# Linear attention with ReGLU on one core: direct values for three tile pairs, Strassen for all keys, values one pair ahead of the keys

## The chip, the cores and the metric

The kernel runs on one core of one Trainium2 chip. The metric is the device time of one execution in microseconds, the smaller the better. PE is the matmul engine, DVE, ACT and POOL are the vector, scalar and general engines, SP issues most transfers. "Product" below means one of the seven products of a Strassen group.

## The reference

The input is 2048 tokens of 1024 features, in bf16. Cut to what matters:

```python
phi = lambda t: jnp.where(t > 0, t + 1, jnp.exp(t)) + 1e-6
qkv = layernorm(x) @ wqkv                       # 1024 -> 3 * 1024
pq, pk = phi(q), phi(k)                          # 32 heads of 32
kv = jnp.einsum("bhsd,bhse->bhde", pk, v)        # sums over all tokens
z = jnp.einsum("bhsd->bhd", pk)
o = num / den                                    # pq @ kv over pq @ z
h = x + o @ wo
# ... second layer norm, gate * relu, up, down: the later 84% of the span, untouched here
```

The change touches only the stage that makes keys and values of all tokens and accumulates `kv`. Queries cannot start before it ends.

## The kernel before

Tokens are taken in 16 tiles of 128, two tiles a pair, eight pairs. A projection of one pair to keys (or to values) is done in one of two ways. The direct way is 32 matmuls of 128x512. The other is one Strassen group: seven products of four matmuls each, 28 in all, bought with sums: four sums of the transposed input per pair on DVE (`x_sums`), and four sums of the weights, made once, on DVE for keys (`TWk`) and on POOL for values (`TWv`, 32 pieces that are put into POOL's queue a few at a time by `pool_piece`).

The group, cut to its order. `SX(i)` is an input sum, `TW(i)` a weight sum, and `hook(i)` a place where other work is issued:

```python
def sgroup(...):
    prod(a, X(0, 0), W(0, 0), True, "P1")
    ident_act(bank(b), bank(a), ...)             # ACT copies PSUM to PSUM
    hook(1)
    prod(f, SX(2), TW(2), True, "P7")            # second product: the first input sum
    ident_act(s7, bank(f), ...)
    hook(2)
    prod(b, SX(1), TW(1), False, "P6")           # third: the third input sum
    ident_act(bank(c), bank(b), ...)             # the fifth product waits for this copy
    hook(3)
    prod(a, X(1, 0), W(1, 0), False, "P2")
    hook(4)
    prod(c, SX(0), TW(0), False, "P5")
    hook(5)
    prod(b, X(1, 1), TW(3), False, "P4")         # sixth: the last weight sum
    hook(6)
    prod(c, SX(3), W(1, 1), False, "P3")
```

The input sums of a pair, four DVE operations with two inputs in SBUF each:

```python
def x_sums(p):
    ...
    add(2, xb(0, 0), xb(0, 1), ALU.subtract, ...)
    add(0, xb(0, 1), xb(1, 1), ALU.add, ...)
    add(1, s(0), xb(0, 0), ALU.subtract, ...)
    add(3, xb(1, 0), s(1), ALU.subtract, ...)
```

The order of the stage, cut. Tiles 0 to 3 get keys and values directly while their inputs and the weights arrive; then each pair gets its keys and at once its values, and the input sums of pair p+1 are made at the end of key group p:

```python
for p in range(WB // 2, NP_):                    # pairs 2 to 7
    def h_k3(p=p): ...  kvacc(st)                # accumulation of the pair before, behind the third product
    def h_k6(p=p, sq=sq):
        ...
        if p + 1 < NP_:
            x_sums(p + 1)                        # used by key group p + 1: a value group lies between
    k_group(p, {1: h_k1, 3: h_k3, 5: h_k5, 6: h_k6})
    if p == WB // 2:
        ...                                      # values of pair 2 directly
        continue
    v_group(p, {3: h_v3, 5: h_v5, 6: h_v6})      # h_v6: normalise two later tiles, transpose them by DMA
```

`kvacc` is the accumulation, 16 matmuls of 128x129 per pair. `W` and `TW` of keys and values live in the tiles that the profile calls `RAB`, `RC` (`TWk`) and `RW` (`TWv`); the transposed input is in `RAB`, the input sums in `RWG` and `RH`, copies in `RX` and `RXH`, keys, values and the input tiles in `RE`.

## Time and profile before

| | before |
|---|---|
| time, median of four runs (range) | 749.56 us (748.96 to 749.98) |
| span of the profiled run | 747.4 us |
| PE busy | 99% |
| first projection matmul | 8.30 us |
| first query group | 120.67 us |
| waits of PE over 0.3 us between these | one, 0.7 us |

These are the span, the engines' busy time, the clock that PE was granted (in tenths, per slice of the span) and the shares of the chain that ended last, from the page of the kernel before:

```profile
span 747.4 us, 10100 instructions
...
PE 737.0 (99%) x3547; PEld 337.8 (45%) x3603; DVE 537.3 (72%) x1067; ACT 299.9 (40%) x516; POOL 87.5 (12%) x148
...
PEclk9999999999999999999999999999999999999999
...
PE 89%; DVE 4%; ACT 3%; issue 2%; SPq 0%; DMA 0%; DVEq 0%; POOL 0%; ACTq 0%; POOLq 0%
```

PE sets the time: it is always busy, at the full clock, and 89% of the chain. So each matmul less is worth its spacing. What that is, a row of the timeline shows. These are PE's rows of one steady key group and the start of its value group, before the change (start, time, what; four matmuls make one product):

```profile
86.37 1.04 PE L604 MATMUL ps<-RAB,RH 128*128 128x512 bf16 x4
87.24 1.03 PE L604 MATMUL ps<-RAB 128*128 128x512 bf16 x4
88.11 2.00 PE L604 MATMUL ps<-RW,RWG 128*128 128x512 f16 x8
89.94 1.03 PE L604 MATMUL ps<-RAB 128*128 128x512 bf16 x4
```

From 86.37 to 87.24 there are four matmuls in 0.87 us. A single one is listed with 379 ns. The Trainium skill ("TensorE: Matmul & The Clock Gate", Back-to-back issue gap) gives, by its formula, about 216 ns from one 512-column matmul to the next at the full clock, and the trace agrees (the 131 ns that the section gives for a sustained stream do not appear here): the 379 ns is a latency that the next one overlaps.

The waits of PE in the stage, in us in total, number, and the longest:

```profile
PE ps L604 <- ACT RAB L731: 0.7, 1, 0.7
```

This is DVE at the same time as the PE rows above, the input sums (L806):

```profile
87.56 0.93 DVE L806 TENSOR_TENSOR RWG<-RAB 128x512 f16<-128x512 bf16 x2
88.52 0.43 DVE L806 TENSOR_TENSOR RWG<-RWG,RAB 128x512 f16<-128x512 f16 x1
88.98 0.42 DVE L806 TENSOR_TENSOR RH<-RAB,RWG 128x512 f16<-128x512 bf16 x1
```

They start 0.32 us after the value group's first product at 87.24, take about 0.45 us each, and are not wanted before the next key group near 94 us. These rows give least, median and greatest duration in ns of the input sums that started between 33 and 51 us, before:

```profile
L806 DVE TENSOR_TENSOR RWG<-RAB x4: 534/884/887, 33.9 to 47.4; 128x512 f16<-128x512 bf16 x4
L806 DVE TENSOR_TENSOR RWG<-RWG,RAB x2: 774/776/778, 35.6 to 48.4; 128x512 f16<-128x512 f16 x2
```

Here POOL adds weights almost without a pause, and one sum takes up to 0.89 us. A whole value projection lies between these sums and their use.

### The profile page before, as it was taken

How to read it: one execution, taken by the hardware profiler on the slowest of the kernel's cores; microseconds unless marked ns; L12 is line 12 of the kernel's file. 1: busy time of each engine (PE TensorE's matmuls, PEld its weight loads, DVE VectorE, ACT ScalarE, POOL GpSimd, SP SyncE). 2: the span in 40 equal slices, each digit the busy share in tenths (PEclk: the TensorE clock that was granted, in tenths of full speed). 3: DMA queues.
4: the chain of work that ended last, by engine and by line, in shares of the span. 5: the costliest groups of instructions: out<-in, count | busy, mean ns of one | idle time of the engine just before them, and what ended most of it. 6: DMA issues, size and time to landing. Idle time of an engine off the chain costs nothing.

```text
span 747.4 us, 10100 instructions
## 1 busy us (share of the span) xinstructions
PE 737.0 (99%) x3547; PEld 337.8 (45%) x3603; DVE 537.3 (72%) x1067; ACT 299.9 (40%) x516; POOL 87.5 (12%) x148
## 2 busy tenths in 40 slices
PE   8999999999999999999999999999999999999998
PEld 4444444344554444444444444444444444444443
DVE  7987875898776899887877485766867677563343
ACT  4367755665832354545443100035454454520000
POOL 2695440000350000000000010000000000000000
PEclk9999999999999999999999999999999999999999
DMA  9734115223898696565428799732323131036663
GB/s 306 200 74 97 29 29 184 84 29 82 219 224 243 222 290 198 172 187 175 143 85 251 224 266 301 234 120 84 105 65 112 58 114 56 1 87 182 211 192 132
DMA packets 160225, 113.38 MB, mean 152 GB/s; under 512 B 51504, under 2 KB 141360, under 8 KB 160176
## 3 DMA queue, kind: packets, MB, share of 16 engines
q1 hardware_dynamic: 160176, 112.75, 52.6%
q8 instruction: 28, 0.46, 0.3%
q14 instruction: 21, 0.17, 0.1%
HBM read 85.46 MB, written 15.73 MB: 135 GB/s over the span
## 4 chain that ended last, share of the span: by engine, by line
PE 89%; DVE 4%; ACT 3%; issue 2%; SPq 0%; DMA 0%; DVEq 0%; POOL 0%; ACTq 0%; POOLq 0%
PE ps L604 89%; DVE RAB L670 1%; ACT ps L609 1%; ACT RX L663 1%; ACT RX L609 1%; DVE RX L667 1%; DVE RE L1038 1%; ACT RXH L633 0%; ACT RXH L638 0%; DVE RX L884 0%; SPq L510 0%; DVE RXH L1062 0%; DMA RW<-in_B_W_down_dram 0%; DVE rden L1036 0%; PE ps L728 0%
## 5 line engine op out<-in xcount | busy, mean ns | idle before, releaser
L609 ACT ACTIVATE ps<-ps 128x512 f32<-128x512 f32 x150 | 87.4, 584 | 172.3 <-PE ps L604 155.6
L604 PE MATMUL ps<-RC,RO 128*128 128x512 f16 x672 | 154.4, 379 | 0.7 <-DVE RE L1219 0.6
L604 PE MATMUL ps<-RW,RAB 128*128 128x512 f16 (+1 forms) x681 | 150.1, 379 | 0.6
L604 PEld LDWEIGHTS ps<-RW,RAB 128*128 128x128 bf16 (+1 forms) x692 | 67.7, 98 | 81.6
L604 PE MATMUL ps<-RH,RWG 128*128 128x512 bf16 x435 | 103.0, 379 | 0.7
L604 PEld LDWEIGHTS ps<-RC,RO 128*128 128x128 f16 x672 | 65.5, 98 | 80.7 <-ACT ps L609 1.1
L609 ACT ACTIVATE RE<-ps 128x512 f32<-128x512 f32 x120 | 70.7, 597 | 75.0 <-PE ps L604 52.8
L604 PE MATMUL ps<-RC,RWG 128*128 128x512 f16 x296 | 70.7, 379 | 0.0
L604 PEld LDWEIGHTS ps<-RH,RWG 128*128 128x128 bf16 x448 | 43.8, 98 | 52.9 <-DVE RAB L1212 0.3
L1212 DVE TENSOR_TENSOR RAB<-ps,RAB 128x512 bf16<-128x512 f32 x28 | 19.3, 690 | 63.3 <-PE ps L604 63.3
L604 PE MATMUL ps<-RH,RO 128*128 128x512 bf16 (+1 forms) x242 | 58.3, 379 | 0.7
L609 ACT ACTIVATE RAB<-ps 128x512 bf16<-128x512 f32 x56 | 33.4, 597 | 61.9 <-PE ps L604 61.8
L604 PE MATMUL ps<-RAB 128*128 128x512 bf16 x239 | 56.6, 379 | 1.3 <-ACT RAB L731 0.7
L604 PE MATMUL ps<-RW,RE 128*128 128x512 bf16 x248 | 56.8, 379 | 0.8 <-DVE RXH L1062 0.4
L1143 DVE TENSOR_TENSOR RO<-RWG,RO 128x512 f16<-128x512 bf16 x108 | 45.5, 421 | 1.8
L604 PEld LDWEIGHTS ps<-RC,RWG 128*128 128x128 bf16 (+1 forms) x296 | 28.5, 98 | 35.7 <-ACT ps L609 2.2
L1143 DVE TENSOR_TENSOR RO<-RWG 128x512 f16<-128x512 bf16 x108 | 40.7, 418 | 2.8 <-DMA RWG<-in_B_W_up_dram 2.1
L625 POOL TENSOR_TENSOR rstd<-rstd,neghalf 128x1 f32<-128x1 f32 x20 | 12.6, 632 | 251.5 <-DVE rstd L622 251.5
L1219 DVE TENSOR_TENSOR RE<-ps,RE 128x512 f32<-128x512 f32 x56 | 38.3, 691 | 5.0 <-ACT RE L609 4.8
L1224 DVE TENSOR_TENSOR RE<-ps,RE 128x512 f32<-128x512 f32 x56 | 38.2, 683 | 0.0
L604 PEld LDWEIGHTS ps<-RH,RO 128*128 128x128 f16 (+1 forms) x256 | 24.6, 98 | 29.8 <-ACT RX L609 1.5
L667 DVE TENSOR_SCALAR RX<-RX 128x512 bf16<-128x512 bf16 x64 | 19.9, 311 | 24.0 <-ACT RX L663 23.9
(118 smaller groups left out, 809.9 us busy)
## 6 DMA issues: line engine op xcount, KB each, us to landing
RWG<-in_B_W_gate_dram SPq DMA_DIRECT2D x28, 512.0 KB, 3.7
RWG<-in_B_W_up_dram SPq DMA_DIRECT2D x28, 512.0 KB, 4.9
RW<-t_scr SPq DMA_DIRECT2D x56, 256.0 KB, 3.1
RW<-in_B_W_down_dram SPq DMA_DIRECT2D x42, 256.0 KB, 4.1
RW<-in_B_W_down_dram SPq DMA_DIRECT2D x14, 512.0 KB, 3.9
t_scr<-RW SPq DMA_DIRECT2D x14, 512.0 KB, 4.9
RE<-in_A_x_dram SPq DMA_DIRECT2D x23, 256.0 KB, 4.3
RAB<-in_A_wqkv_dram SPq DMA_DIRECT2D x8, 512.0 KB, 7.8
```

The lines of the kernel that those rows point to most:

```text
L604: lambda e: e.matmul(out_ap, lhsT, rhs, start=start, stop=stop, skip_group_check=skip),
L609: PL.add("act", lambda e: e.activation(out=dst, in_=src, func=func), reads=reads, writes=writes, name=name)
L625: PL.add("pool", lambda e: e.tensor_tensor(out=rstd[:, k, :], in0=rstd[:, k, :], in1=neghalf[:], op=ALU.pow), reads=[B_neghalf], writes=[B ...
L663: PL.add("act", lambda e: e.activation(out=Et[:, k, :], in_=src, func=ACTF.Exp), reads=[src_buf], writes=[B_E[k]], name=name + "_exp")
L667: PL.add("dve", lambda e: e.tensor_scalar(out=Et[:, k, :], in0=Et[:, k, :], scalar1=1.0, scalar2=1e-6, op0=ALU.min, op1=ALU.add), reads=[] ...
L670: PL.add("dve", lambda e: e.scalar_tensor_tensor(out=dst_ap, in0=src, scalar=C1, in1=Et[:, k, :], op0=ALU.add, op1=ALU.max), reads=[src_bu ...
L1038: PL.add("dve", lambda e: e.tensor_tensor(out=osb[:, k, :].rearrange("p (g h e) -> p g h e", h=HPG, e=Dh), in0=nv[:, :, 0:P].rearrange("p ...
L1143: PL.add(eng, lambda e: e.tensor_tensor(out=Tring[:, k, j], in0=in0, in1=in1, op=ALU.subtract), reads=reads, writes=[B_T[k][j]], name="T%d ...
L1212: PL.add("dve", lambda e: e.tensor_tensor(out=hh[:, f1, 0:SBW], in0=bank(BA[1]), in1=r11[:, rr, :], op=ALU.mult), reads=[B_bank[BA[1]], B_ ...
L1219: PL.add("dve", lambda e, w=w: e.tensor_tensor(out=ftmp[:, 4 + w, :], in0=bank(BF_[w]), in1=ftmp[:, 2 + w, :], op=ALU.add), reads=[B_bank[ ...
L1224: PL.add("dve", lambda e, w=w: e.tensor_tensor(out=ftmp[:, 6 + w, :], in0=bank(BB[w]), in1=ftmp[:, w, :], op=ALU.add), reads=[B_bank[BB[w] ...
```

## The change

The intent is to spend fewer matmuls. Keys of pairs 0 and 1 become Strassen groups (two groups of 28 in place of 64), all keys now use the weight sums that exist already, and values of pairs 0, 1 and 2 go first and directly. With pair 2's values direct in both, the stage has 96 direct matmuls and 13 groups in place of 160 and 11: 460 in place of 468. The values of pair p+2 follow the keys of pair p, so six value slots are kept, and only two key slots. The accumulation of a pair moves into a later value group. The core of the diff:

```diff
-        NPK = 4
+        NPK = 2
+        NV = 6
...
+        v_piece(0, 0, lambda: T1(1))
+        v_piece(1, 0, lambda: T1(2))
+        x_sums(0)
+        ln1_norm(3)
+        pool_q += w_sums("pool", wv_, bw_v, tw_v, B_TWv, "TWv", 1, NW // 2)
+        v_piece(2, 0, lambda: T1(3))
...   # TWk on DVE between the other direct value pieces; norms of tiles 4 and 5
-            def h_k3(p=p):
-                for st in (2 * p - 2, 2 * p - 1):
-                    if st >= WB - 1:
-                        kvacc(st)
...
-                if p + 1 < NP_:
-                    x_sums(p + 1)
+                if 3 <= p + 2 < NP_:
+                    x_sums(p + 2)
+            return {1: k1, 5: k5, 6: k6}
...
+        k_group(0, kv_hooks(0))
+        v_piece(4, 0, lambda: run_pend(1))
+        run_pend(2)
+        v_piece(4, 1, lambda: run_pend(3))
+        pool_piece(3)
+        x_sums(1)
+        v_piece(5, 0)
+        pool_piece(3)
+        norms(3)
+        v_piece(5, 1)
+        x_sums(2)
+        pool_piece(6)
+        kvaccs(0)
+        for p in range(1, NP_):
+            hooks = kv_hooks(p)
+            if p == NP_ - 1:
+                hooks[5] = lambda h5=hooks[5]: (h5(), kvaccs(NP_ - 2))
+            k_group(p, hooks)
+            if p + 2 < NP_:
+                v_group(p + 2, {3: pp, 5: pp, 6: lambda p=p: (norms(p + 3), kvaccs(p))})
...
-                    hooks[3] = lambda: (kvacc(NST - 2), kvacc(NST - 1))
+                    hooks[6] = lambda: kvaccs(NP_ - 1)
```

`x_sums(p + 2)` is issued at the end of key group p, and value group p+2 comes next and uses it at once. The slack of a whole group that the sums had is gone.

More of the change, by code (lines that the diff above doesn't have):

```diff
@@ L249, in bass_sequential_preLN__linear_attn_block__glu_gated_reglu__prompt_kernel @@
         hnT = RH[:].rearrange("p (a b) -> p a b", a=NDC)
-        RE = sb("RE", [P, NX1 * D + NPK * D + NPK * NG * VW], bf16)
+        RE = sb("RE", [P, NX1 * D + NPK * D + NV * NG * VW], bf16)
         x1 = RE[:, 0:NX1 * D].rearrange("p (a b) -> p a b", a=NX1)
@@ L255, in bass_sequential_preLN__linear_attn_block__glu_gated_reglu__prompt_kernel, with pk_slot, pk_ap @@
         o0 += NPK * D
-        vv = RE[:, o0:o0 + NPK * NG * VW].rearrange("p (a g w) -> p a g w", a=NPK, g=NG)
+        vv = RE[:, o0:o0 + NV * NG * VW].rearrange("p (a g w) -> p a g w", a=NV, g=NG)
+        def pk_slot(st):
+            return st % NPK if st < NST - 2 else NPK + st % 2
+        def pk_ap(st):
+            i = pk_slot(st)
+            return pk[:, i, :] if i < NPK else x1[:, i - NPK, :]
         osb = RE[:, 0:NO * D].rearrange("p (a b) -> p a b", a=NO)
@@ L372, in bass_sequential_preLN__linear_attn_block__glu_gated_reglu__prompt_kernel @@
         B_wo = bufs("wo_", ND2)
-        B_pk = [bufs("pk%d_" % i, ND2) for i in range(NPK)]
-        B_v = [bufs("v%d_" % i, ND2) for i in range(NPK)]
+        B_pk = [bufs("pk%d_" % i, ND2) for i in range(NPK + 2)]
+        B_v = [bufs("v%d_" % i, ND2) for i in range(NV)]
         B_E = bufs("E_", NPH)
@@ L423, in flat @@
             return [b for row in x for b in (flat(row) if isinstance(row, list) else [row])]
+        for i in range(2):
+            for b_ in B_pk[NPK + i]:
+                b_.over = B_x1[i]
         kv_ring = flat(B_x1) + flat(B_pk) + flat(B_v) + [B_vones]
@@ L611, in bass_sequential_preLN__linear_attn_block__glu_gated_reglu__prompt_kernel, with ln_stats_steps, bn, fin @@
         stat_ctr = [0]
-        def ln_stats(src_full, src_chunk_bufs, name):
+        def ln_stats_steps(src_full, src_chunk_bufs, name):
             k = stat_ctr[0] % NSTAT
             stat_ctr[0] += 1
-            for c in range(NBC):
-                PL.add("dve", lambda e, c=c: e.bn_stats(out=st6[:, k, c * 6:(c + 1) * 6],
-                                                        in_=src_full[:, c * BCH:(c + 1) * BCH]),
+            def bn(c):
+                PL.add("dve", lambda e: e.bn_stats(out=st6[:, k, c * 6:(c + 1) * 6],
+                                                   in_=src_full[:, c * BCH:(c + 1) * BCH]),
                        reads=[src_chunk_bufs[c]], writes=[B_st6[k][c]], name=name + "_bn")
-            PL.add("dve", lambda e: e.bn_aggr(out=mv[:, k, :], in_=st6[:, k, :]),
-                   reads=B_st6[k], writes=[B_mv[k]], name=name + "_aggr")
-            PL.add("dve", lambda e: e.tensor_scalar(out=rstd[:, k, :], in0=mv[:, k, 1:2], scalar1=EPS,
-                                                    scalar2=None, op0=ALU.add),
-                   reads=[B_mv[k]], writes=[B_rstd[k]], name=name + "_ve")
-            PL.add("pool", lambda e: e.tensor_tensor(out=rstd[:, k, :], in0=rstd[:, k, :], in1=neghalf[:],
-                                                     op=ALU.pow),
-                   reads=[B_neghalf], writes=[B_rstd[k]], name=name + "_rstd")
+            def fin():
+                PL.add("dve", lambda e: e.bn_aggr(out=mv[:, k, :], in_=st6[:, k, :]),
+                       reads=B_st6[k], writes=[B_mv[k]], name=name + "_aggr")
+                PL.add("dve", lambda e: e.tensor_scalar(out=rstd[:, k, :], in0=mv[:, k, 1:2], scalar1=EPS,
+                                                        scalar2=None, op0=ALU.add),
+                       reads=[B_mv[k]], writes=[B_rstd[k]], name=name + "_ve")
+                PL.add("pool", lambda e: e.tensor_tensor(out=rstd[:, k, :], in0=rstd[:, k, :], in1=neghalf[:],
+                                                         op=ALU.pow),
+                       reads=[B_neghalf], writes=[B_rstd[k]], name=name + "_rstd")
+            return k, [lambda: bn(0), lambda: bn(1), fin]
+        def ln_stats(src_full, src_chunk_bufs, name):
+            k, steps = ln_stats_steps(src_full, src_chunk_bufs, name)
+            for f_ in steps:
+                f_()
             return k
@@ L700, in ln1_stats, with ln1_steps @@
             ln1_k[st] = ln_stats(x1[:, i, :], B_x1[i], "ln1_%d" % st)
+        def ln1_steps(st):
+            i = st % NX1
+            ln1_k[st], steps = ln_stats_steps(x1[:, i, :], B_x1[i], "ln1_%d" % st)
+            return steps
         def ln1_stats_act(st):
@@ L717, in ln1_norm @@
                 ln_norm_dve(ln1_k.pop(st), x1[:, i, :], B_x1[i], xn[:, st % NXN, :], B_xn[st % NXN], "ln1_%d" % st)
-            if st + NX1 < NST:
+            if 6 <= st + NX1 < NST:
                 load_x1(st + NX1)
@@ L747, in pe_dummies, with v_piece @@
                 mm(bank(b, 512), zeros_t[:, 0:P], zeros_t, True, True, [B_zeros], B_bank[b], "dummy")
-        def kvp_piece(st, nt, mid=None):
-            slot = st % NPK
+        def v_piece(st, h, mid=None):
             b = alloc_bank(P1_POOL)
+            nt = ND2 + h
             for dc in range(NDC):
-                if dc == NDC // 2 and mid is not None:
+                if mid is not None and dc == NDC // 2:
                     mid()
@@ L756, in kvp_piece @@
                    dc == 0, dc == NDC - 1, [xnT_buf(st, dc), B_wkv[nt][0 if dc < WKH else 1]], B_bank[b],
-                   "kvp_%d_%d" % (st, nt))
-            if nt < ND2:
-                phi(bank(b), B_bank[b], pk[:, slot, nt * NW:(nt + 1) * NW], B_pk[slot][nt], "k_%d_%d" % (st, nt))
-            else:
-                v_copy(b, st, nt - ND2)
+                   "v_%d_%d" % (st, h))
+            v_copy(b, st, h)
         def v_out(st, j):
-            return vv[:, st % NPK, j * GPN:(j + 1) * GPN, 0:P]
+            return vv[:, st % NV, j * GPN:(j + 1) * GPN, 0:P]
         def gw(ap):
@@ L770, in v_copy @@
             PL.add("act", lambda e: e.activation(out=v_out(st, j), in_=gw(bank(b)), func=ACTF.Identity),
-                   reads=[B_bank[b]], writes=[B_v[st % NPK][j]], name="v_%d_%d" % (st, j))
+                   reads=[B_bank[b]], writes=[B_v[st % NV][j]], name="v_%d_%d" % (st, j))
         def w_sums(eng, wsrc, bw, tw, btw, name, chunk, cw=NW):
@@ L927, in dst @@
             def dst(t, h):
-                sl = (2 * p + t) % NPK
-                return pk[:, sl, h * NW:(h + 1) * NW], B_pk[sl][h]
+                st = 2 * p + t
+                return pk_ap(st)[:, h * NW:(h + 1) * NW], B_pk[pk_slot(st)][h]
             def pl(t, h):
@@ L946, in go @@
                                                                             op=ALU.add),
-                                           reads=[pb, sb_], writes=[B_v[sb2 % NPK][j]], name="v_%d_%d" % (sb2, j))]
+                                           reads=[pb, sb_], writes=[B_v[sb2 % NV][j]], name="v_%d_%d" % (sb2, j))]
                 return go
@@ L952, in vc @@
                                                                                    func=ACTF.Identity),
-                                                     reads=[bb], writes=[B_v[sa % NPK][j]], name="v_%d_%d" % (sa, j))]
+                                                     reads=[bb], writes=[B_v[sa % NV][j]], name="v_%d_%d" % (sa, j))]
             sgroup(P1_POOL, True, X, SX, W, TW, vc(0), vc(1), va(0), va(1), "v%d" % p, hooks)
@@ L983, in kvacc @@
         def kvacc(st):
-            slot = st % NPK
+            sv = st % NV
+            pa = pk_ap(st)
             for g in range(NG):
@@ L989, in kvacc @@
                 kv_started[kb] = True
-                mm(kv_out(g), pk[:, slot, g * P:(g + 1) * P], vv[:, slot, g, 0:P + 1],
-                   first, st == NST - 1, [B_pk[slot][half], B_v[slot][half], B_vones], B_bank[kb],
+                mm(kv_out(g), pa[:, g * P:(g + 1) * P], vv[:, sv, g, 0:P + 1],
+                   first, st == NST - 1, [B_pk[pk_slot(st)][half], B_v[sv][half], B_vones], B_bank[kb],
                    "kvacc_%d_%d" % (st, g), skip=True)
@@ L1375, in down_pass @@
                     n[0] += 1
-        WB = 4
         load_x1(0, split=True)
-        load_wkv(0, half=0)
+        load_x1(1)
         act_warm()
-        load_x1(1)
-        load_wkv(0, half=1)
+        load_wkv(2, half=0)
         load_x1(2)
-        load_wkv(1)
-        load_x1(3)
-        late_wkv = [2, 3]
-        pe_dummies(12, P1_POOL)
-        ln1_stats(0)
-        ln1_norm(0)
-        load_wkv(late_wkv.pop(0))
-        ln1_stats(1)
-        for st in range(WB):
-            T1(st)
-            if st == 0:
-                pe_dummies(3, [alloc_bank(P1_POOL)])
-            ln1_norm(st + 1)
-            if st + 1 >= WB:
-                T1d(st + 1)
-            if st == 0:
-                while late_wkv:
-                    load_wkv(late_wkv.pop(0))
-                pool_q += w_sums("pool", wv_, bw_v, tw_v, B_TWv, "TWv", 1, NW // 2)
-            ln1_stats(st + 2)
-            if st >= 2:
-                kvp_piece(st - 2, 1)
-            kvp_piece(st, 0)
-        pool_piece(6)
+        load_wkv(2, half=1)
+        load_x1(3)
+        load_wkv(3)
+        pe_dummies(12, P1_POOL)
+        s0, s1_, s2_, s3 = [ln1_steps(st) for st in range(4)]
+        for f_ in s0 + s1_[:1]:
+            f_()
+        ln1_norm(0)
+        load_wkv(1)
+        T1(0)
+        pe_dummies(3, [alloc_bank(P1_POOL)])
+        for f_ in s1_[1:] + s2_[:1]:
+            f_()
+        ln1_norm(1)
+        load_x1(4)
+        load_x1(5)
+        load_wkv(0)
+        for f_ in s2_[1:] + s3[:1]:
+            f_()
+        ln1_norm(2)
+        for f_ in s3[1:]:
+            f_()
+        v_piece(0, 0, lambda: T1(1))
[4 more added lines that the diff above has]
+        v_piece(2, 0, lambda: T1(3))
+        v_piece(0, 1)
+        twk = w_sums("dve", wkv, bw_k, tw_k, B_TWk, "TWk", KH)
+        twk.pop(0)()
+        v_piece(3, 0)
+        ln1_stats(4)
+        twk.pop(0)()
+        ln1_norm(4)
+        T1d(4)
+        pool_piece(4)
+        v_piece(1, 1)
+        m5, q5 = ln1_stats_act(5)
+        m5()
+        twk.pop(0)()
+        v_piece(2, 1)
+        q5()
+        ln1_norm(5)
+        T1d(5)
+        pool_piece(8)
+        twk.pop(0)()
+        v_piece(3, 1)
         for i in range(2):
@@ L1411, in bass_sequential_preLN__linear_attn_block__glu_gated_reglu__prompt_kernel, with kv_hooks, k1 @@
         pool_q += w_sums("pool", wq, bw_q, TWq, B_TWq, "TWq", 1, NW // 2)
-        for st in range(WB - 2, WB):
-            kvp_piece(st, 1)
-        ln1_norm(WB + 1)
-        T1d(WB + 1)
-        ln1_stats(WB + 2)
-        pool_piece(4)
-        for f_ in w_sums("dve", wkv, bw_k, tw_k, B_TWk, "TWk", KH):
-            f_()
-        for nt in range(2, NKV):
-            for st in range(WB):
-                kvp_piece(st, nt)
-                if nt == 2 and st == 2:
-                    x_sums(WB // 2)
-                if nt == 2 and st == 3:
-                    ln1_norm(WB + 2)
-                    T1d(WB + 2)
-                    ln1_stats(WB + 3)
-                if nt == NKV - 1 and st == 2:
-                    ln1_norm(WB + 3)
-                    T1d(WB + 3)
-                if nt == NKV - 1 and st >= 1:
-                    kvacc(st - 1)
-                pool_piece(2)
         NP_ = NST // 2
-        for p in range(WB // 2, NP_):
+        def kv_hooks(p):
             sq = []
-            A, B = 2 * p + 4, 2 * p + 5
-            few = p < NP_ - 2
-            def h_k1(p=p, A=A):
+            A, B = 2 * p + 6, 2 * p + 7
+            def k1():
                 pool_piece(2)
@@ L1444, in h_k1, with k5 @@
                     ln1_stats(A)
-                else:
-                    x_sums(p - NP_ + 2)
-            def h_k3(p=p):
-                for st in (2 * p - 2, 2 * p - 1):
-                    if st >= WB - 1:
-                        kvacc(st)
-            def h_k5(B=B, sq=sq):
+            def k5():
                 pool_piece(2)
@@ L1458, in h_k5, with k6, norms, kvaccs @@
                     sq.append(q_)
-            def h_k6(p=p, sq=sq):
+            def k6():
                 for f_ in sq:
                     f_()
-                if p + 1 < NP_:
-                    x_sums(p + 1)
-            def h_v3(few=few):
-                if not few:
-                    pool_piece(2)
-            def h_v5():
-                pool_piece(2)
-            def h_v6(A=A, B=B):
-                for st in (A, B):
-                    if st < NST:
-                        ln1_norm(st)
-                        T1d(st)
-            k_group(p, {1: h_k1, 3: h_k3, 5: h_k5, 6: h_k6})
-            if p == WB // 2:
-                for f_ in pend.pop(1):
-                    f_()
-                kvp_piece(2 * p, 2)
-                for f_ in pend.pop(2):
-                    f_()
-                kvp_piece(2 * p, 3)
-                for f_ in pend.pop(3):
-                    f_()
-                h_v5()
-                kvp_piece(2 * p + 1, 2)
-                h_v6()
-                kvp_piece(2 * p + 1, 3)
-                h_v5()
-                continue
-            v_group(p, {3: h_v3, 5: h_v5, 6: h_v6})
+                if 3 <= p + 2 < NP_:
+                    x_sums(p + 2)
+            return {1: k1, 5: k5, 6: k6}
+        def norms(p):
+            for st in (2 * p, 2 * p + 1):
+                if st < NST:
+                    ln1_norm(st)
+                    T1d(st)
+        def kvaccs(p):
+            kvacc(2 * p)
+            kvacc(2 * p + 1)
+        def pp():
+            pool_piece(2)
+        k_group(0, kv_hooks(0))
+        def run_pend(i):
+            for f_ in pend.pop(i, ()):
+                f_()
+        v_piece(4, 0, lambda: run_pend(1))
[17 more added lines that the diff above has]
+                v_group(p + 2, {3: pp, 5: pp, 6: lambda p=p: (norms(p + 3), kvaccs(p))})
         assert not pool_q
```

## The prediction

> **What bounds it now.** In the busy table PE has 99% of the 747.4 us span; the chain of waits puts 89% on PE; the clock row is full. The 379 ns per matmul is latency, not spacing: the Trainium skill ("TensorE: Matmul & The Clock Gate", Single matmul latency and Back-to-back issue gap) gives (398+512)/2.4 = 379 ns and about 216 ns start to start. The timeline agrees: four matmuls per 0.866 us, 0.2165 us each. The change touches the key/value stage, by the timeline from the first real matmul at 8.30 us to the first query group at 120.67 us. PE has one wait over 0.3 us there (0.73 us before 11.37, for ACT's eviction of the second transposed tile).
>
> **What changes on PE.** Before: 160 direct matmuls and 11 Strassen groups of 28 (six key, five value). After: 96 direct and 13 groups (eight key, five value): 468 -> 460, 8 x 0.2165 = **-1.73 us**, all critical. Transposes and KV accumulation keep their counts. The query stage and all after it (84% of the span) stay.
>
> **What is added.** Two key groups bring 8 ACT copies (0.58 us) and 4 DVE adds (0.69 us); ACT and DVE are 50 to 80% busy there, so only the waits of PE matter:
> - KV accumulation moves from behind the third product of a key group to before the last product of a value group. Its 0.94 us hid the copy that the fifth product needs. Value groups show a 0.26 us gap there, because exponentials of the previous key group stand ahead of the copy on ACT. Key groups after value groups have none, so I expect 0.05 us in seven of them, 0.26 us in the last, 0.08 us in the first query group: **+0.6 us**.
> - The sums of pair p+2 are now made at the end of key group p and used at once by value group p+2; before, a whole group lay between. They start 0.32 us after the value group (87.56 against 87.24), 0.46 us each; the second product wants one at +0.87, the third the third sum (ready at +1.8) at +1.74. About 0.15 us per value group, five groups: **+0.7 us**.
> - Start: transposes inside the direct value pieces should remove the 0.73 us wait, but DVE does the sums of pair 0 (1.8 us) before normalising tile 3, whose transpose I estimate 0.5 us late: **-0.2 us** net.
> - Weight sums on DVE (1.2 and 1.6 us each) precede the first key group at about 24 us. wkv should land by 20 us (5.8 MB at the windows' 350 GB/s). The last sum waits behind a normalisation with late statistics from ACT: done near 27.6, needed at 28.4. **+0.1 us**.
> - Two key slots suffice: accumulation of p is issued before key group p+1 evicts.
>
> Sum: about -0.5; I lean slightly lower, since waits overlap: **748.6 us**, range **746.8 to 750.4**. Chances: faster by over 2% 0.01, within 2% 0.98, slower 0.01.
>
> **What would show it.** Right: 8 fewer 512-column matmuls; first query group at 119.5 to 120.5 us; later stages only shifted; in value groups, PE weight loads released by DVE sums at the second or third product; no gap near 11, a small one near 14. Wrong: key groups over 6.3 us without accumulation; a PE gap at 24 to 29 us released by weight sums or a wkv DMA; value groups without DVE-released gaps (then nearer 747.5).
>
> **What would make it wrong.** The chain of sums on DVE slipping by a microsecond (its operations slow from 0.42 to 0.77 us while POOL adds run); POOL's value weight sums (32 adds of 0.7 to 0.84 us) not done by the first Strassen value group near 44 us; late x loads in the first 8 us.

## The result, and the profile after

| | before | after |
|---|---|---|
| time, median of four runs (range) | 749.56 us (748.96 to 749.98) | 752.11 us (751.50 to 753.44) |
| span of the profiled run | 747.4 us | 750.0 us |
| first projection matmul | 8.30 us | 7.73 us |
| first query group | 120.67 us | 122.73 us |
| steady pair (keys, values, accumulation) | 13.56 us | 13.55 us |

The ratio is 1.0037, with a 95% interval of 1.0020 to 1.0054. Ratios here are the mean time of one kernel's fast runs over that of the other's of the same rounds, so not quite the ratio of the medians. The result correctly stayed within 2%, but it is 1.7 us above the upper end of the predicted range, on the other side of the time before. The kernel with eight matmuls fewer is slower.

The same lines of the page after:

```profile
span 750.0 us, 10163 instructions
...
PE 739.3 (99%) x3595; PEld 335.1 (45%) x3595; DVE 538.4 (72%) x1063; ACT 308.0 (41%) x532; POOL 89.9 (12%) x152
...
PE 87%; DVE 6%; ACT 3%; issue 2%; DMA 1%; SPq 1%; DVEq 0%; POOL 0%; ACTq 0%
```

The counts are no sign against the change: PE has 3595 records in place of 3547 because some matmul records are missing from the first trace. The weight loads, one for each matmul, are 3603 and 3595: eight fewer.

The page hides the matter: PE is still at 99%, and the shares of the chain hardly moved: DVE grew from 4% to 6%, DMA and SP's queue to 1% each. The waits of PE between 7 and 123 us show it:

```profile
PE ps L616 <- DVE RWG L829: 2.2, 1, 2.2
PE ps L754 <- DVE RXH L673: 1.0, 2, 0.7
PE ps L616 <- issue: 0.5, 1, 0.5
...
```

L829 is an input sum (L806 of before). The largest is a single wait, and the PE rows after the change say where: in the first Strassen value group, that of pair 3. In brackets stands the idle time before, and what ended it ("issue": nothing that the profile shows):

```profile
44.47 1.03 PE L616 MATMUL ps<-RAB 128*128 128x512 bf16 x4
47.70 1.02 PE L616 MATMUL ps<-RW,RWG 128*128 128x512 f16 x4 [2.20 <-DVE RWG L829]
49.27 1.02 PE L616 MATMUL ps<-RW,RWG 128*128 128x512 f16 x4 [0.55 <-issue]
...
54.86 0.38 PE L616 MATMUL ps<-RAB 128*128 128x512 bf16 x1
```

The group takes 10.39 us, from 44.47 to 54.86. The later value groups take 7.27 to 7.37 us, most of them 7.36, the accumulation included. So this one group costs 3.03 us more, nearly twice what the eight matmuls give. The next fence is DVE over the 9 us in front of its second product, and on to the third input sum:

```profile
38.01 0.96 DVE L673 TENSOR_SCALAR RXH<-RE,mv,rstd 128x1024 bf16<-128x1024 bf16 x1
38.89 0.89 DVE L739 TENSOR_SCALAR RXH<-RE,s 128x1024 bf16<-128x1024 bf16 x1
39.70 1.70 DVE L829 TENSOR_TENSOR RWG<-RAB 128x512 f16<-128x512 bf16 x2
41.43 0.78 DVE L829 TENSOR_TENSOR RWG<-RWG,RAB 128x512 f16<-128x512 f16 x1
42.24 0.77 DVE L829 TENSOR_TENSOR RH<-RAB,RWG 128x512 f16<-128x512 bf16 x1
...
44.56 0.62 DVE L688 TENSOR_SCALAR RX<-RX 128x512 bf16<-128x512 bf16 x1
45.21 0.69 DVE L691 SCALAR_TENSOR_TENSOR RE<-ps,RX 128x512 bf16<-128x512 f32 x1
...
46.42 0.68 DVE L907 TENSOR_TENSOR RXH<-ps,RXH 128x512 f32<-128x512 f32 x1
47.02 1.34 DVE L829 TENSOR_TENSOR RWG<-RAB 128x512 f16<-128x512 bf16 x2
48.40 0.77 DVE L829 TENSOR_TENSOR RWG<-RWG,RAB 128x512 f16<-128x512 f16 x1
```

No row has a bracket, nor has one of those left out: DVE never waits. It is a queue that is behind. The sums of pair 3 start at 47.02, which is 2.55 us after the group's first product, where the prediction had taken 0.32 us. The third sum ends at 49.17, and the third product, which reads it, starts at 49.27: this is the wait of 0.55 us that the profile could not put down to anything. The four sums of pair 2 took 3.25 us (1.70 + 0.78 + 0.77), against 1.8 us in the steady rows of before. The four sums of pair 1, just before, took 1.60 us from 36.42 on, when POOL had only statistics of one column to do. POOL explains why, perhaps; here is its row of the time, 14 additions of weights without a pause:

```profile
38.02 10.87 POOL L804 TENSOR_TENSOR RW<-RAB,RW 128x256 f16<-128x256 bf16 x14
```

A caution about reading: the row of weight loads of the waiting product reads "2.66 <-POOL RW L804", so it names POOL instead. A POOL addition happened to end at that moment, but the additions of that time make `TW(3)`, which only the sixth product needs. The first sum of pair 3 ended at about 47.6 us as well (half of the 1.34 us from 47.02), and it is what the product reads. A releaser in a profile is an inference and has to be checked against who reads what.

Two of the four runs had a mean granted clock of 0.998, and these are the slower two (752.55 and 753.44 us, against 751.67 and 751.50). The experiments come back to this.

### The profile page after: what moved, and what is told of

The parts are those of the page before. It is cut to its first block, busy times and chain, and to the rows that moved or that the text cites. A ratio compares the mean times of both kernels' runs of the same rounds, so it can differ in the third digit from the quotient of the medians.

```text
span 750.0 us, 10163 instructions
## 1 busy us (share of the span) xinstructions
PE 739.3 (99%) x3595; PEld 335.1 (45%) x3595; DVE 538.4 (72%) x1063; ACT 308.0 (41%) x532; POOL 89.9 (12%) x152
## 4 chain that ended last, share of the span: by engine, by line
PE 87%; DVE 6%; ACT 3%; issue 2%; DMA 1%; SPq 1%; DVEq 0%; POOL 0%; ACTq 0%
PE ps L616 87%; DVE RAB L691 1%; ACT ps L621 1%; DMA RE<-in_A_x_dram 1%; DVE RX L688 1%; ACT RXH L654 1%; ACT RXH L659 1%; SPq L522 1%; DVE RE L1062 1%; DVE RX L907 0%; ACT RX L684 0%; ACT RX L621 0%; DVE RWG L829 0%; DVE RE L691 0%; DMA RW<-in_B_W_down_dram 0%
## 5 line engine op out<-in xcount | busy, mean ns | idle before, releaser
L621 ACT ACTIVATE ps<-ps 128x512 f32<-128x512 f32 x154 | 89.7, 583 | 182.1 <-PE ps L616 163.3
L616 PE MATMUL ps<-RH,RWG 128*128 128x512 bf16 x448 | 106.0, 379 | 0.3 <-DVE RAB L1236 0.3
L616 PE MATMUL ps<-RC,RWG 128*128 128x512 f16 x320 | 76.6, 380 | 0.1
L616 PE MATMUL ps<-RH,RO 128*128 128x512 bf16 (+1 forms) x256 | 61.2, 379 | 0.0
L616 PE MATMUL ps<-RAB 128*128 128x512 bf16 x200 | 48.1, 379 | 0.1
L616 PEld LDWEIGHTS ps<-RC,RWG 128*128 128x128 bf16 (+1 forms) x320 | 30.0, 98 | 39.9 <-ACT ps L621 5.9
L616 PEld LDWEIGHTS ps<-RW,RE 128*128 128x128 bf16 x256 | 24.5, 98 | 28.0 <-DVE RXH L1086 0.7
```

Source lines behind the costliest of these rows:

```text
L616: lambda e: e.matmul(out_ap, lhsT, rhs, start=start, stop=stop, skip_group_check=skip),
L621: PL.add("act", lambda e: e.activation(out=dst, in_=src, func=func), reads=reads, writes=writes, name=name)
```

## The experiments

All ratios are against the kernel before, in the same rounds. Kernels with a prefix e are correct. Those with f or g are for measuring only and give wrong results on purpose. In the texts letters stand for theories; the text after each names in words the one that held.

The theory at first: the first Strassen value group waits because DVE comes to the sums of pair 3 late, behind the sums of pair 2, which aren't needed before key group 2 (theory A). A rival: POOL's weight sums come at their own pace and bind anyway (theory B). Another: what was lost is elsewhere (the start, the moved accumulation), and the stall only takes slack from later work.

### Sums of pair 2 moved behind those of pair 3

```diff
         v_piece(5, 1)
-        x_sums(2)
...
-  v_group(p + 2, {3: pp, 5: pp, 6: ...})
+  v_group(p + 2, {3: pp, 4: (lambda p=p: x_sums(2) if p == 1 else None), 5: pp, 6: ...})
```

> Only move: the input sums of pair 2 go from the end of the direct pieces of pair 2 to the middle of the first Strassen value group (pair 3), so 3.3 us of DVE work leaves the stretch in front of the sums of pair 3. Theory A (the 3.2 us lost in the first Strassen value group come from DVE's order alone): its gaps close, first query group at about 119.6 us instead of 122.7, time about 749.0. Theory B (POOL's 32 value weight sums, which ended at 51.1 us, bound the same group from behind): the gap moves from the second product to the sixth, its weight load is released by POOL, and only 1 to 1.5 us is won: about 750.8.

Measured: 751.55 us (750.63 to 751.80), ratio 1.0029 (1.0014 to 1.0044). The waits of PE in this kernel between 40 and 66 us:

```profile
PE ps L616 <- POOL RW L804: 1.3, 1, 1.3
PE ps L616 <- ACT RX L684: 0.5, 1, 0.5
PE ps L616 <- DVE RWG L829: 0.3, 1, 0.3
```

The wait for the input sum at the second product is gone, and most of it has come back as a wait of 1.3 us at the sixth, for the last sum of weights on POOL, which ends near 51 us in both kernels. In the kernel after, the stall in front had hidden this. The 0.5 us, at the third product, is put down to ACT, but the third input sum ends at 46.52 us, 0.10 us before that product starts: DVE's sums are still slow (1.24, 0.77 and 0.78 us). So both theories hold in turn: DVE's queue binds first, and POOL's pace right behind it. The time missed both expectations, 749.0 and 750.8.

### Six weight sums issued to POOL earlier, and both together

```diff
         pool_q += w_sums("pool", wv_, bw_v, tw_v, B_TWv, "TWv", 1, NW // 2)
+        pool_piece(6)
         v_piece(2, 0, lambda: T1(3))
...
         x_sums(2)
-        pool_piece(6)
         kvaccs(0)
```

> Only move: six of POOL's value weight sums start in its idle time near 13 us instead of near 38 us. POOL then ends the value weight sums about 4 us earlier and no longer slows the DVE at the end of that stretch. Theory A (DVE's order alone): the gap before the second product of the first Strassen value group stays above 1.5 us, time 751.2 to 752. Theory B alone (POOL late): the whole gap closes, about 749. Theory C (DVE is late because POOL's adds slow its own operations, 0.42 to 0.77 us): the pair 3 sums start about 1 us earlier, and half of the loss goes, about 750.5.

Measured: 751.95 us, ratio 1.0033 (1.0016 to 1.0050). The gap before the second product stayed, 2.14 us, and the sums of pair 3 started at 47.11. Giving POOL a lead alone does nothing, as the chain of DVE in front is the same: eight additions still run beside it from 38.45 to 44.7 us, and the sums of pair 2 take 3.24 us. So this was no test of the theory that POOL's additions slow DVE (theory C). The sums of pair 3, which now have only POOL's statistics beside them, take 1.59 us in place of 2.53. In the profiled run the clock fell to about half right after the gap (eight matmuls from 47.66 on took 3.02 us).

> Both moves of the two runs before. If DVE's order and POOL's pace each bind (A and B), only this one closes the group's gaps: first query group at about 119.7 us, about 749.0, and better than each alone by about 1 us. If A alone holds, equal to the first; if B or C alone, equal to the second.

Measured: 752.83 us, ratio 1.0047 (1.0033 to 1.0062): a miss. The gaps of the group of pair 3 shrank to 0.52, 0.36 and 0.33 us. But key group 2 got a gap of 0.77 us (an ACT copy), the next value group one of 1.70 us with 1.53 us of it for an input sum, and the two gaps at the start came to about 1 us each. The work that DVE was spared in one place stood in the way in the next.

### Values of pair 3 directly

```diff
+            if p == 1:
+                run_pend(1)
+                v_piece(6, 0, lambda: run_pend(2))
+                run_pend(3)
+                v_piece(6, 1)
+                pool_piece(2)
+                v_piece(7, 0)
+                norms(4)
+                v_piece(7, 1)
+                pool_piece(2)
+                kvaccs(1)
-            if p + 2 < NP_:
+            elif p + 2 < NP_:
                 v_group(...)
```

> Values of pair 3 directly too, which need neither the sums of pair 3 nor the value weight sums: four more matmuls (0.87 us), but nothing to wait for. If the stall of the first Strassen value group is all that the change lost, first query group near 120.2 us, time 749.3 to 749.8, and the next value group (pair 4) shows no gap over 0.3 us. If the lateness of DVE and POOL is only passed on, the pair 4 group shows a gap of over 1 us and the time stays over 751.

Measured: 749.90 us (749.71 to 750.56), ratio 1.0011 (0.9996 to 1.0026). It has four matmuls more (0.87 us), and by the ratios it is 2.0 us faster than the kernel after (0.0026 of 749.5 us). The sum of the two, 2.8 us, is nearly the 3.03 us of the group. The stall is gone, and the group of pair 4 has no gap over 0.3 us, as expected; one wait of 1.1 us of the accumulation for the keys remains, and the first query group starts at 120.96 us, near the 120.67 us of before. So the loss lies in the group of pair 3, not at the start and not in the moved accumulation.

### A weight sum ahead of a normalisation, and every reordering together

> Only move: the last of DVE's four key weight sums goes ahead of the normalisation of tile 5, so DVE works through the 2.6 us that it idled for POOL's statistics near 23 to 25.7 us. Theory D (that idle time is where DVE's lateness began): the sums of pair 3 start 1 to 1.7 us earlier than at 47.0, the gap before the second product of the first Strassen value group shrinks from 2.4 to about 1 us; about 751.3. Theory E (DVE is held again later, by POOL's statistics for tile 7, which are ready only at 38.05 us, so an earlier start is lost): sums of pair 3 start within 0.4 us of 47.0 and the time stays at 751.8 to 752.3.

The edit issues the last `TWk` sum before `ln1_norm(5)`. Measured: 752.37 us, ratio 1.0043 (1.0028 to 1.0057). The sums of pair 3 started at 46.92 us, where they were: the head start was lost before 34 us, where DVE now waited 0.67 and 0.20 us for ACT. In three of four runs the clock was 0.998. In the profiled one the clock can be seen to fall. The columns: the window in us, its length and PE, PEld, DVE, ACT and POOL busy, then the granted clock, the DMA share and GB/s:

```profile
46.00:48.00 2.00, 0.40 (x2) 0.22 (x3) 2.00 (x4) 1.09 (x2) 1.83 (x3) 1.00 0.00 0
48.00:50.00 2.00, 1.45 (x6) 0.39 (x5) 1.90 (x5) 1.11 (x2) 1.94 (x3) 0.67 0.03 8
50.00:52.00 2.00, 2.00 (x6) 0.72 (x5) 1.85 (x3) 0.56 (x2) 1.78 (x4) 0.50 0.00 0
52.00:54.00 2.00, 2.00 (x10) 0.88 (x9) 1.33 (x2) 1.69 (x4) 1.80 (x3) 0.98 0.02 4
```

The stretch had two gaps, of 2.48 and 0.72 us by the spacing of the matmuls, with one product between them; after it PE ran at half the clock for some 3 us. The profiled run of the kernel after had nearly the same gaps (2.36 and 0.70 us) and kept the full clock. So the loss can grow by a microsecond or two by chance: a mean clock of 0.998 over 750 us is an estimated 1.5 us of lost clock, and the two slower runs of the kernel after lie 1.4 us above the two others in the mean.

> The sums of pair 2 later, six POOL sums early, the last key weight sum earlier, and the normalisation of tile 3 before the sums of pair 0. If the loss is DVE's backlog plus POOL's pace (as in the runs so far: closing one gap opened the next, 1.5 us in the second value group when both were eased), the four together leave under 1 us in the first two value groups: 749.0 to 750.0. If a fixed amount of DVE work is simply too much for this stretch, over 1.5 us of gaps stay somewhere in 45 to 65 us: 751 or more. The gap before the transpose of tile 3 (0.73 us at 14.4) should close.

This kernel has the moved sums of pair 2, the early POOL sums, the `TWk` sum in front, and `ln1_norm(3)` in front of `x_sums(0)`. Measured: 751.68 us (750.60 to 751.82), ratio 1.0031 (1.0018 to 1.0043). The gap at 14.4 us closed, as expected. The group of pair 3 had 0.82, 0.23 and 0.34 us left, but key group 2 had the gap of 0.77 us again, and the next value group waited 1.42 us for its input sums. There DVE itself was waiting for the DMA that transposes the tiles of that pair, of which the second had been normalised only at 54.55 to 55.09 us:

```profile
60.65 0.76 DVE L829 TENSOR_TENSOR RWG<-RAB 128x512 f16<-128x512 bf16 x2 [1.57 <-DMA RAB<-RXH]
```

Reordering moves the wait between products and groups; it does not remove it. It looked as if there were too much for DVE before about 50 us; whether that is so is tested below.

### The accumulation back in its old place

```diff
+            hooks[3] = lambda p=p: kvaccs(p - 1)
             k_group(p, hooks)
...
-  ... 6: lambda p=p: (norms(p + 3), kvaccs(p))})
+  ... 6: lambda p=p: (norms(p + 3))})
```

> Only move: the accumulation of pair p stands again behind the third product of a key group (the next one, before it writes the same key slots), as it did before the change. My prediction gave 0.6 us to the move away from there. If right: no gap of 0.26 us in the last key group and the first query group, the key groups' small gaps filled, the stage 0.5 to 0.7 us shorter, time about 751.5; the stall of the first Strassen value group unchanged within 0.3 us. If the accumulation's place does not matter: 752.1.

Measured: 758.86 us (755.94 to 760.09), ratio 1.0124 (1.0108 to 1.0140): far from the expectation. A steady pair took 13.56 us, with no gain over 13.55, so the predicted 0.6 us for the moved accumulation had no place there. And it showed why the change moved it. These are the waits of PE between 110 and 140 us:

```profile
PE ps L616 <- DVE RE L691: 3.8, 4, 1.6
```

Where two groups that need `phi` follow each other (key groups 6 and 7, key group 7 and the first query group), the accumulation behind the third product needs keys whose evictions are still running, and waits 1.62 us each time. That was a fault of this experiment's design. In the profiled run of this kernel the clock fell too, after each of the two waits (0.50 at 122 to 124 us, 0.54 at 132 to 134 us), and three of the four runs have a mean clock of 0.993 to 0.995. The one at full clock (755.94 us) is 4.4 us above the two such runs of the kernel after; the four waits make 3.8 us of it.

> A candidate that could beat both: values of pair 3 directly too (four matmuls more, 0.87 us), accumulation back behind the third product of key groups, last key weight sum earlier, normalisation of tile 3 before the sums of pair 0. From the direct run (749.9): minus 0.7 (start), minus 1.1 (accumulation waiting for DVE), minus 0.5 (accumulation as filler): about 747.7, ratio to the kernel before 0.998. If the gains do not add, 749 to 750.

Values of pair 3 directly, the accumulation in its old place, the `TWk` sum and the norm of tile 3 in front. Measured: 754.69 us in six runs, ratio 1.0075 (1.0062 to 1.0089), another miss (747.7 expected) from the same fault: 1.62 us twice at 118 and 128 us, and 0.77 us for a transposing DMA at 44.7 us.

### What makes DVE late: its own sums, or POOL

By now the queue of DVE was the cause of the stall. Two theories of its length remained: it has too many operations of its own (the sums of pairs 1 and 2 come on top of normalisations), or its operations are slow while POOL adds (theory P). The Trainium skill ("SBUF — State Buffer", Who interferes with whom) says that a DVE instruction with two SBUF inputs contends with a POOL instruction that reads SBUF. The first kernel moves the sums of pairs 1 and 2 to the last two key groups and lets their groups read those of pair 0, a wrong result:

```diff
-        x_sums(1)
...
-        x_sums(2)
...
+                elif p >= NP_ - 2:
+                    x_sums(p - 5)
```

> Wrong result on purpose: the input sums of pairs 1 and 2 (5 us of DVE work between 36 and 44 us) move to the last two key groups, and key groups 1 and 2 read the sums of pair 0. Theory W (too much DVE work in this stretch): the first two Strassen value groups lose at most 0.5 us, first query group near 119.5, about 749. Theory P (POOL's weight sums and POOL's statistics, and the transpose that waits for them, bind by themselves): 1.3 us or more stay at the sixth product, released by POOL, as when the sums of pair 2 were moved: about 750.5 to 751.

Measured: 751.51 us, ratio 1.0033 (1.0020 to 1.0047). The group of pair 3 lost 0.7 us in place of 2.4 at its largest gap, but the sums that were put late delayed the last key evictions, and the accumulation waited for them: a gap of 1.67 us at 120.20 us, an effect of the experiment. It doesn't decide: it shows only that with 5 us of sums less in front, DVE is in time for the second product, whatever made those 5 us. The second kernel leaves POOL's value weight sums out and lets value groups read those of the keys, a wrong result too:

```diff
-        pool_q += w_sums("pool", wv_, bw_v, tw_v, B_TWv, "TWv", 1, NW // 2)
+        pool_q += [lambda dep: None] * 32
...
-            W, TW = w_ops(wv_, bw_v, tw_v, B_TWv)
+            W, TW = w_ops(wv_, bw_v, tw_k, B_TWk)
```

> Wrong result on purpose: POOL makes no value weight sums (32 adds of about 0.75 us from 20 to 51 us); the value groups read the key weight sums. Same DVE and PE work. Theory P (POOL binds, directly, by slowing DVE's operations, and by its late statistics): DVE's sums go back to 0.42 to 0.47 us each, the sums of pair 3 start before 45.3 us and all gaps over 0.3 us of the first Strassen value group go: first query group near 119.5 to 119.9, time 748.7 to 749.3. Theory W (DVE's own work is too much): the sums of pair 3 start after 46 us, a gap over 1 us stays, time over 750.5.

Measured: 749.08 us (748.72 to 749.12), ratio 0.9999 (0.9984 to 1.0014). DVE in this kernel, to be held against the DVE rows after the change:

```profile
37.39 0.54 DVE L673 TENSOR_SCALAR RXH<-RE,mv,rstd 128x1024 bf16<-128x1024 bf16 x1
37.84 0.54 DVE L739 TENSOR_SCALAR RXH<-RE,s 128x1024 bf16<-128x1024 bf16 x1
38.30 0.75 DVE L829 TENSOR_TENSOR RWG<-RAB 128x512 f16<-128x512 bf16 x2
39.09 0.42 DVE L829 TENSOR_TENSOR RWG<-RWG,RAB 128x512 f16<-128x512 f16 x1
39.54 0.42 DVE L829 TENSOR_TENSOR RH<-RAB,RWG 128x512 f16<-128x512 bf16 x1
...
43.03 0.29 DVE L688 TENSOR_SCALAR RX<-RX 128x512 bf16<-128x512 bf16 x1 [1.43 <-ACT RX L684]
...
45.20 0.77 DVE L829 TENSOR_TENSOR RWG<-RAB 128x512 f16<-128x512 bf16 x2
```

The same operations in the same order, and DVE now has 1.43 us to spare. The sums of pair 2 take 1.59 us in place of 3.25, the two normalisations 1.08 in place of 1.85, one step of `phi` 0.29 in place of 0.62: 2.76 us less. The sums of pair 3 start 0.31 us after the first product (44.89), as the prediction had taken from the steady state, and no gap of the group is over 0.33 us. So DVE's own count of operations is not too large; beside POOL's additions it becomes so. The first query group came at 120.21 us, 0.3 us later than expected; this run also began later (first projection matmul at 8.06 us, then a DMA wait of 0.38).

> Both of the two runs before (wrong result on purpose). Under either theory no gap over 0.3 us is left in the value groups: this is the floor that my prediction assumed: first query group 119.3 to 119.7, time 748.4 to 749.2. If it stays over 750, what the change lost is not in this stretch.

With both edits: 750.81 us, ratio 1.0020 (1.0007 to 1.0034). No value group had a gap over 0.33 us, and the side effect of the late sums was there again, 1.66 us at 119.61 us, so the expected time was missed for that reason.

One thing was still open: without POOL's sums, POOL's queue is also short, and the statistics of the norms that pass through it come sooner. That could have been the cause in place of contention. So the last kernel keeps POOL as busy in the same queue, but with fills of 128x768, which write and read nothing, about as long (0.81 us) as the additions:

```diff
+        def fake(j):
+            def go(dep=None):
+                PL.add("pool", lambda e: e.memset(RW[:, 0:768], 0.0), writes=B_TWv, deps=[dep], name="fake")
+            return go
+        pool_q += [fake(i // 8) for i in range(32)]
```

> Wrong result on purpose: as the run without POOL's sums (value groups read the key weight sums), but POOL stays as busy: each of the 32 adds becomes a fill of 768 elements, which writes to the same memory and reads nothing (about 0.7 to 0.8 us each by the fill of 512 at the start, 0.52 us). Theory S (DVE is late because POOL's reads hold the port that DVE's two-input sums need): the input sums stay at 0.42 to 0.47 us each, only single-input bf16 operations (normalisations, minimum step) may still be slowed, the sums of pair 3 start before 45.8 us (0.3 of it start jitter), the gap before the second product is under 0.5 us, and the time is 749 to 749.6. Theory Q (DVE is late because POOL's queue delays the statistics of tiles 6 and 7): POOL's queue is as long as before, the sums of pair 3 start after 46.5 us, a gap over 1.5 us stays, time over 750.8.

Measured: 748.54 us (748.44 to 749.77), ratio 0.9986 (0.9970 to 1.0003). POOL, and then DVE, in its profile:

```profile
38.29 11.45 POOL L1435 MEMSET RW<- 128x768 bf16 x14
```

```profile
37.83 0.54 DVE L673 TENSOR_SCALAR RXH<-RE,mv,rstd 128x1024 bf16<-128x1024 bf16 x1
38.45 0.89 DVE L739 TENSOR_SCALAR RXH<-RE,s 128x1024 bf16<-128x1024 bf16 x1
39.26 0.74 DVE L829 TENSOR_TENSOR RWG<-RAB 128x512 f16<-128x512 bf16 x2
40.03 0.43 DVE L829 TENSOR_TENSOR RWG<-RWG,RAB 128x512 f16<-128x512 f16 x1
...
45.98 0.75 DVE L829 TENSOR_TENSOR RWG<-RAB 128x512 f16<-128x512 bf16 x2
```

POOL is just as full (14 instructions in 11.45 us, against 10.87), and the input sums are at their short time again, while an operation with one bf16 input, such as the second normalisation, still takes 0.89 us at times. The sums of pair 3 start 0.76 us after the first product (45.22), in place of 2.55, and 0.20 us of wait is left. The time is a little below the expected 749 to 749.6, and the profiled run is the slowest of the four (749.77). This is the theory of POOL's reads (S); that of a long POOL queue (Q) is refuted. That it is the reads, and not another part of the additions, rests on the page: the fills leave out both. Neither this kernel nor the one before it has a real weight sum that a value group waits for, so both also take away the wait that would come next, that for `TW(3)`.

### A version for use

> Correct candidate: values of pair 3 directly too (0.87 us more matmuls), so that neither the sums of pair 3 nor POOL's weight sums are due before about 59 us; accumulation of pair 1 behind the third product of key group 2; tile 3 normalised before the sums of pair 0; four fewer POOL sums ahead of the statistics of tile 6. From 749.9 of the direct run: minus 0.7 at the start, minus 1.1 for the accumulation: 748.1; ratio to the kernel before 0.9985. If another wait takes their place (the transposes of tiles 6 and 7 for the direct pieces), 749 to 750.

Values of pair 3 directly, the accumulation of pair 1 behind the third product of key group 2, the norm of tile 3 before the sums of pair 0, and four POOL sums fewer in the first direct part. It is correct. Measured: 749.53 us (748.92 to 749.62), ratio 1.0005 (0.9992 to 1.0017). The 748.1 that was expected was missed, and the second guess (749 to 750) held: it is equal to the kernel before, with four matmuls fewer than it. No version was found that beats it.

## Why the prediction was wrong

The sum of the prediction, with what the profiled runs showed:

| term | predicted, us | measured, us |
|---|---|---|
| eight matmuls fewer | -1.73 | -1.73 (460 of 468, same spacing) |
| accumulation moved | +0.6, mostly in seven key groups | about +0.56 (+0.45 in the last key group, +0.32 in five others, -0.20 in the value groups), and +0.20 later, in the first query group |
| input sums used at once | +0.7, 0.15 in each value group | +3.03 in the first; in the others 0.10 at the second product, made up by smaller gaps (row above) |
| start | -0.2 | 0.0 (first matmul 0.57 earlier, gaps before 15 us as much more: after 32 matmuls both stand at about 17.45 us) |
| weight sums on DVE | +0.1 | no gap |
| two more Strassen groups have small gaps of their own | not counted | +0.18 (28 x 0.216 = 6.05; groups of 6.09 and 6.19; 32 direct matmuls in a row have none) |
| first query group, by the trace | -0.5 for all terms | +2.06 |

- **The step that failed** is, as the prediction put it, "About 0.15 us per value group, five groups: +0.7 us". It rested on sums that start 0.32 us after the group's first product and take 0.46 us each, read at 87 us, where POOL's additions are sparse. At the first Strassen value group they started 2.55 us after it, since POOL adds without a pause from 38 us on and the sums in front of them take 0.77 us and more each. The kind of wait was right: in the later groups the second product does wait for its sum, but 0.10 us (62.02 against 61.92), and the steady pair lost nothing (13.55 us, against 13.56 us). The size was wrong where POOL adds: the first group lost 3.03 us. The prediction named the slow sums and POOL's weight sums under what would make it wrong, and gave them no place in the sum. The trace of before already had the durations at the right time: 0.53 to 0.89 us at 34 to 49 us.
- **The matmuls** were right: they are all critical, and all were delivered. When the stall is taken away by force (0.9999 without POOL's sums, 0.9986 with fills), the change is worth between nothing and about 1 us by the ratios, and both intervals include no gain at all.
- **The accumulation** came to the predicted size partly by luck. The 0.05 us for a key group was right: key groups 1 to 6 take 6.19 to 6.20 us without it, against 6.14 before (7.08 less 0.94 for the accumulation). But the value groups, which hold it now, lose 0.06 us less than before (7.36 less 0.94, against 6.48), which the prediction did not have, so a steady pair pays nothing. The last key group takes 6.59 us, and the first query group 7.29 in place of 7.09: both more than predicted.
- **The start** was right in kind, with a wait of 0.73 us near 14 us (0.5 predicted), which the kernel with every reordering removed. But it gained nothing in place of 0.2 us, as there is a second wait, 0.32 us at 9.08.
- **The range** had been too narrow: a sum of small terms was given a certainty that its largest term, taken from a wrong place, could not bear.

The terms measured add up to +2.04 us, against +2.06 us at the first query group; they are read by the spacing of the matmuls, and each may be off by a few hundredths. Behind that mark the spans differ by 0.5 us more, of which the first query group has 0.20. It is also open what decides whether a gap lowers the clock, and why the first transfers land at slightly different times from run to run.

## What to carry to other kernels

An operation's duration has to be read from the stretch of the trace in which the changed kernel will run it, not from the steady state: the same DVE sum took 0.42 us and 0.77 to 0.89 us in one trace, according to what POOL did. A change that brings a producer next to its consumer removes slack, and then the slowest occurrence of the producer counts, not the mean one. An engine at 99% busy does not show a stall of 3 us in 750: the waits by line and the gaps of the one group do.

## What the Trainium skill lacked or had wrong

- "SBUF — State Buffer", Who interferes with whom: it is right that a DVE instruction with two SBUF inputs contends with POOL instructions that read, and not with those that only write: 0.42 us against 0.77 us with additions, 0.42 us with fills. It gives no figure for sums like these. Here a 128x512 sum of two inputs grew by 0.35 us and more under additions of about 0.78 us that follow each other (14 in 10.87 us).
- The same section says that the form with one input (`tensor_scalar`) can contend in its two-port mode. The runs agree, with fills too: the 128x1024 normalisation took 0.54 us alone, and 0.89 us beside fills.
- "TensorE: Matmul & The Clock Gate", What's actually happening: it ties the slow clock to an idle window of about 3.4 us. Here gaps of 2.5 and 0.7 us with matmuls between them, in a second kernel a single gap of 2.1 us, and in a third one of 1.6 us (after one of 0.3), were followed by some 3 us at half the clock in the profiled execution (granted clock 0.50 to 0.54 over 2 us), while other executions of the same kernels have a mean clock of 1.000.
- No page gives the time from the end of a tile's normalisation to the landing of its DMA transpose (128x1024 bf16, issue and queue included). In the kernel with every reordering it was about 5.6 us, from 55.09 to 60.65 us, where the sum that waits for it starts; 2.0 us of this passed before SP issued the transpose, at 57.05.
